# Attention backward of a decode block: dk/dv on the full array, K/V in 8 KB rows, and SP's queue ordered as loads, stores, zeros

## The chip, the core and the metric

The kernel runs on one core of a Trainium2 chip. The metric is the device time in microseconds. Five engines take part: PE (TensorE), DVE (VectorE), ACT (ScalarE), POOL (GpSimd) and SP (SyncE). Each runs its own instructions in order, and each but PE and DVE also issues transfers here, which 16 DMA engines carry out.

## The reference

The reference is the forward pass and all gradients of one decode step: windowed attention with a cache, in parallel with a GEGLU feed-forward block, both on the layer-normed x. There are 4 rows (B = 4), D = 512, 32 query heads over 8 K/V heads of 128, a cache of 4096 positions of which the last W = 1024 are used, F = 1792. Everything is bf16.

```python
xn = layernorm(x)
q = (xn @ wq) per head;  k, v = cache[:, :, Sk-W:], each shared by 4 heads
p = softmax(q k^T / sqrt(128));  o = p v
out = x + o @ wo + (gelu(xn @ w_gate) * (xn @ w_up)) @ w_down
# and the vjp with grad_out: dx, dk_cache, dv_cache, dwq, dwo, dw_gate, dw_up, dw_down
```

The outputs make the traffic. dk_cache and dv_cache (out_2, out_3) have the full 4096 positions: 3072 of each are zeros, 48 MiB in all, and 1024 are computed, 16 MiB in all. K and V are read over 1024 positions (16 MiB), and the weights and their gradients add the rest. The profile counts 30.93 MB read and 81.01 MB written.

## The kernel before

The kernel works in two parts. First comes the feed-forward block (lines 479 to 628): gate, up and down weights are loaded whole, `hg_ps` and `da_ps` are computed, then a loop of 14 steps (the df loop, L614 to L626) transposes the gate and up weights for dx. Then the attention runs in NT = 4 stages of GP = 2 K/V heads each, with 8 query heads for 4 rows, hence 32 pairs of row and head.

A stage t (the loop of L632) goes so. `pre(t)` transposes wo, computes q and the gradient of o, and writes them into `qm` and `dom`, in which each block has the columns of one row and K/V head and zeros elsewhere. `masks(t)` makes masked copies of the two as rows for the outer products (POOL). `scores(t, 0)` transposes K in blocks of 8 x 128x128, copies each block from PSUM with one DVE operation of 1024 columns, and adds up the scores S on 128 partitions: 4 quarters of the window by 32 pairs. `softmax(t)` follows; then `scores(t, 1)` does the same with V and gives dP. `softmax_d(t)` makes dS. `odq` multiplies P by V and dS by K. `fin(t)` transposes wq and adds to the sums for out and dx.

The outer products are cut into pieces that wait in a list `bg`: a piece is one or two matmuls into one PSUM bank and one evacuation of 512 columns. `tick(n)` takes n pieces off the list, between transposes. `dvdk(t, k)` puts 16 pieces for dv or dk on the list, `dw(t)` 16 for dwo and dwq; the feed-forward block leaves 46. In a piece of dk/dv (L406) the contraction runs over one quarter, 32 of the 128 rows of the array. `evac` shares the evacuations between ACT and DVE by a running sum of costs.

Transfers: SP issues x, dy, the feed-forward weights, wo and wq of stages 0 and 1, K/V of stage 0 and half of stage 1, and then `zeros()`: all 32 transfers of 1.5 MiB of zeros, each held until the second before it has landed. ACT issues the later K/V and wo/wq loads (`load_next`, `load_w`), between its evacuations. POOL issues the stores. K and V lie in the tiles as [128 positions mod 8, row, 8 positions, 128], so a partition takes 2 KB from each of the 4 rows. Only SP's order is written by hand (`manual_schedule`); the order of the other engines is a scheduler's.

PSUM pools are `ps_w` (4 banks, shared by transposes, pieces and sums), `ps_a` (S, dP and od) and `ps_x` (1 bank). The staging tiles of dk/dv are 4, those of the other gradients (`outp`) 3.

Of the kernel before, what the change touches and what calls it, by code (L numbers as in the profile page):

```python
# [9 lines left out]
ACT = mybir.ActivationFunctionType  # L10
# [4 lines left out]
P = 128  # L15
# [3 lines left out]
def kernel(  # L19
# [23 lines left out]

    nc = tc.nc
# [11 lines left out]
    J = W // P  # L56
# [3 lines left out]
    RG = B * HG  # L60
    NQ = P // RG
    WQ = W // NQ
    JQ = J // NQ
    NS = B * GP
    CW = HG * Dh
    assert Sq == 1 and Dh == P and D == 512 and F % P == 0 and RG == 32 and JQ * NQ == J and WQ == JQ * P
# [4 lines left out]
    kvp = ctx.enter_context(tc.tile_pool(name="kvp", bufs=3))  # L71
    wres = ctx.enter_context(tc.tile_pool(name="wres", bufs=2))
    attw = ctx.enter_context(tc.tile_pool(name="attw", bufs=2))
    tsb = ctx.enter_context(tc.tile_pool(name="tsb", bufs=5))
# [4 lines left out]
    ctx.enter_context(tc.manual_schedule(engines={nc.sync.engine}))  # L79
# [14 lines left out]
    def store(eng, out, in_, kind, apart):  # L94

        d = eng.dma_start(out=out, in_=in_)  # L96
        for k in apart:
            tc.declare_no_dep(d.ins, group=k, reason="stores write disjoint parts of the outputs")
        tc.add_to_no_dep_group(kind, d.ins)
        return d  # L100


    RB = P // B
    x_b = const.tile([P, D], BF16, name="x_b")
    dy_b = const.tile([P, D], BF16, name="dy_b")
    for dst, src in ((x_b, A_x), (dy_b, grad_out)):
        nc.sync.dma_start(out=dst[:], in_=bass.AP(tensor=src.tensor, offset=src.offset,
                                                  ap=[[D, B], [0, RB], [1, D]]))

    ident = const.tile([P, P], BF16, name="ident")  # L110
    make_identity(nc, ident[:])
    ident_f = const.tile([P, P], FP32, name="ident_f")
    nc.vector.tensor_copy(out=ident_f[:], in_=ident[:])
    one_f = const.tile([1, 1], FP32, name="one_f")
    nc.vector.memset(one_f[:], 1.0)

    msk_i = const.tile([P, rep], FP32, name="msk_i")
    nc.vector.reduce_sum(out=msk_i[:], in_=ident_f[:].rearrange("p (b r) -> p r b", b=B)[:, 0:rep, :], axis=AX.X)


    rsum = const.tile([P, NQ, RG], FP32, name="rsum")
    nc.gpsimd.memset(rsum[:], 1.0)

    msk_f = const.tile([P, GP, B], FP32, name="msk_f")
    nc.gpsimd.memset(msk_f[:], 1.0)
    for q in range(NQ):
        rs = slice(q * RG, (q + 1) * RG)
        nc.gpsimd.affine_select(out=rsum[rs], in_=rsum[rs], pattern=[[0, NQ], [-1, RG]],
                                compare_op=ALU.is_equal, fill=0.0, base=0, channel_multiplier=1)
        nc.gpsimd.affine_select(out=msk_f[rs], in_=msk_f[rs], pattern=[[-rep, GP], [-HG, B]],  # L130
                                compare_op=ALU.is_ge, fill=0.0, base=0, channel_multiplier=1)
        nc.gpsimd.affine_select(out=msk_f[rs], in_=msk_f[rs], pattern=[[rep, GP], [HG, B]],
                                compare_op=ALU.is_ge, fill=0.0, base=rep - 1, channel_multiplier=-1)
    msk = const.tile([P, GP, B], BF16, name="msk")
    nc.vector.tensor_copy(out=msk[:], in_=msk_f[:])

    ZW = K0 // P * Dh
    ztile = const.tile([P, ZW], BF16, name="ztile")
    nc.vector.memset(ztile[:], 0.0)

    qm_all, dom_all = [], []
    for i in range(2):
        for lst, nm in ((qm_all, "qm"), (dom_all, "dom")):
            t_ = const.tile([P, NS, RG + rep], BF16, name=f"{nm}{i}")
            nc.gpsimd.memset(t_[:], 0.0)
            lst.append(t_)


    acc = const.tile([P, 2, ND, B], FP32, name="acc")
    nc.vector.memset(acc[:], 0.0)  # L150

# [3 lines left out]
    def acc_sum(o, terms):  # L155

        ps = ps_w.tile([P, ND, B], FP32, name="acc_ps", tag="w")
        for c in range(ND):
            for k, (lf, rhs) in enumerate(terms):
                nc.tensor.matmul(ps[:, c, :], lhsT=lf(c), rhs=rhs, start=(k == 0), stop=(k == len(terms) - 1))  # L160
        acc_add(o, ps[:])


    od_ps = ps_a.tile([P, 2, GP, Dh], FP32, name="od_ps")
    nc.vector.memset(od_ps[:], 0.0)


    stats = const.tile([P, nc.vector.BN_STATS_DIM], FP32, name="stats")
    nc.vector.bn_stats(out=stats[:], in_=x_b[:])
    mv = const.tile([P, nc.vector.BN_AGGR_DIM], FP32, name="mv")  # L170
    nc.vector.bn_aggr(out=mv[:], in_=stats[:])
    eps_t = const.tile([P, 1], FP32, name="eps_t")
    nc.vector.memset(eps_t[:], eps)
    rstd = const.tile([P, 1], FP32, name="rstd")
    nc.scalar.activation(out=rstd[:], in_=mv[:, 1:2], func=ACT.Sqrt, bias=eps_t[:], scale=1.0)
    nc.vector.reciprocal(out=rstd[:], in_=rstd[:])
    xn_f = const.tile([P, D], FP32, name="xn_f")
    nc.vector.tensor_scalar(out=xn_f[:], in0=x_b[:], scalar1=mv[:, 0:1], scalar2=rstd[:, 0:1],
                            op0=ALU.subtract, op1=ALU.mult)
    xn_b = const.tile([P, D], BF16, name="xn_b")  # L180
    nc.vector.tensor_copy(out=xn_b[:], in_=xn_f[:])

    xnT = const.tile([P, ND, B], BF16, name="xnT")
    dyT = const.tile([P, ND, B], BF16, name="dyT")
    for src, dstT in ((dy_b, dyT), (xn_b, xnT)):
        tps = ps_x.tile([P, ND, P], BF16, name="tps", tag="x")
        for c in range(ND):
            nc.tensor.transpose(tps[:, c, :], src[:, c * P:(c + 1) * P], ident[:])
        nc.vector.tensor_copy(out=dstT[:], in_=tps[:].rearrange("p c (b r) -> p c b r", b=B)[:, :, :, 0])


    xnm = const.tile([P, rep, D], BF16, name="xnm")
    dym = const.tile([P, rep, D], BF16, name="dym")
    for src, dst in ((dy_b, dym), (xn_b, xnm)):
        for i in range(rep):
            nc.vector.tensor_scalar(out=dst[:, i, :], in0=src[:], scalar1=msk_i[:, i:i + 1], scalar2=None,
                                    op0=ALU.mult)


    wo_v = A_wo.rearrange("(t h p) n -> t p h n", p=P, h=HG)  # L200
    wq_v = A_wq.rearrange("(c p) (t j) -> t p c j", p=P, j=CW)
    wo_t, wq_t, k_t, v_t = {}, {}, {}, {}

    def load_w(t, eng):
        wo_t[t] = wres.tile([P, HG, D], BF16, name="wo_sb", tag="wo")
        eng.dma_start(out=wo_t[t][:], in_=wo_v[t])
        wq_t[t] = wres.tile([P, ND, CW], BF16, name="wq_sb", tag="wq")
        eng.dma_start(out=wq_t[t][:], in_=wq_v[t])  # L208

    def load_kv(t, k, g, eng):  # L210
        d_, src, nm = ((k_t, A_k_cache, "kb"), (v_t, A_v_cache, "vb"))[k]
        tl = kvp.tile([P, B, J, Dh], BF16, name=nm, tag=nm)
        eng.dma_start(out=tl[:].rearrange("p b j d -> p b (j d)"),  # L213
                      in_=src[:, t * GP + g, K0:Sk, :].rearrange("b (m j) d -> m b (j d)", j=J))
        d_[(t, g)] = tl

    def load_next(t, k):

        if t + 1 < NT:
            load_kv(t + 1, k, 1, nc.scalar)  # L220
        if t + 2 < NT:
            load_kv(t + 2, k, 0, nc.scalar)


    ZG = 2
    zlist = [(og, b, g) for b in range(B) for g in range(0, G, ZG) for og in (out_2, out_3)]

    def zeros():

        zsrc = bass.AP(tensor=ztile.tensor, offset=ztile.offset, ap=[list(ztile[:].ap[0]), [0, ZG], [1, ZW]])  # L230
        done = []
        for og, b, g in zlist:
            z = store(nc.sync, og[b, g:g + ZG, 0:K0, :].rearrange("g (m j) d -> m g (j d)", m=P), zsrc, "zeros",
                      ["rest"])
            if len(done) >= 2:
                tc.add_manual_dep(z.ins, done[-2].ins.name,
                                  mybir.DependencyInfo(mybir.DependencyClass.Sync, mybir.DependencyReason.DATA))
            done.append(z)
# [7 lines left out]


    st = {}

    def pre(t):  # L250

        wo_sb, wq_sb = wo_t[t], wq_t[t]
        dq_ps = ps_x.tile([P, 2, HG, B], FP32, name="doq_ps", tag="x")
        for h2 in range(HG // 2):
            wT_ps = ps_w.tile([P, 2, ND, P], BF16, name="woT_ps", tag="w")
            for i in range(2):
                for c in range(ND):
                    nc.tensor.transpose(wT_ps[:, i, c, :], wo_sb[:, 2 * h2 + i, c * P:(c + 1) * P], ident[:])  # L258
            woT = tsb.tile([P, 2, ND, P], BF16, name="woT", tag="wT")
            evac(woT[:], wT_ps[:], 1024, half=True)  # L260
            for i in range(2):
                for c in range(ND):
                    nc.tensor.matmul(dq_ps[:, 0, 2 * h2 + i, :], lhsT=woT[:, i, c, :], rhs=dyT[:, c, :],
                                     start=(c == 0), stop=(c == ND - 1))
            tick(2)
        for h in range(HG):
# [445 lines left out]
```

## Time and profile before

| what | value |
|---|---|
| median of 3 runs | 316.91 us (312.36 to 318.90) |
| span of the profiled execution | 311.7 us |
| PE, DVE, ACT, POOL busy | 224.1, 146.3, 113.4, 51.3 us |
| mean clock granted to TensorE | 0.738 of full speed |
| moved by DMA | 112.38 MB, mean 361 GB/s over the span |
| q1 (SP), q10 (ACT), q0 (POOL) | 66.59, 14.69, 30.67 MB |

The profiled execution has no time of its own beside its span; what lies around it is seen from the fastest run, 0.7 us above the span, and the slowest, 7.2 us above it. An engine's busy share is an average over stages with different limits. What ends last is read from the slices of the span, from stretches with their DMA rate and clock, and from the chain of waits. A clock of 0.50 means that matmuls in that stretch took about twice as long.

### The profile page before, as it was taken

Reading aid. Unit: us, or ns where it says so; the run is one execution under the profiler, and the core shown is the slowest. Engines: PE = TensorE matmul, PEld = TensorE weight load, DVE = VectorE, ACT = ScalarE, POOL = GpSimd, SP = SyncE. Lnnn points to the kernel's source line nnn. Section 1 sums busy time; section 2 is a strip of 40 time slices with the busy share of each in tenths; the row PEclk is TensorE's granted clock in tenths of the full one; section 3 lists DMA queues with packets and bytes.
Section 4 is the critical chain, followed back from the end, with each engine's and each line's share of the span. In section 5 each row is a group of like instructions: output and inputs, shape, how many; then the busy total and the mean of one; then the engine's idle time right before and its main releaser. Section 6 shows DMA issues by size and latency. Waiting matters only on the chain.

```text
span 311.7 us, 6831 instructions
## 1 busy us (share of the span) xinstructions
PE 224.1 (72%) x2950; PEld 144.7 (46%) x2956; DVE 146.3 (47%) x304; ACT 113.4 (36%) x217; POOL 51.3 (16%) x76
## 2 busy tenths in 40 slices
PE   1269986936988379779648069969789755979861
PEld 0259874615555244465425044455556333756231
DVE  5246663523743234537414025546545424564766
ACT  3010645613613045346022044435244414533650
POOL 6000121610100005201000004201000501110140
PEclk9998998875975555779955555679955559895585
DMA  5999999999999999999999999998999999431494
GB/s 167 397 351 385 374 402 416 416 422 424 419 295 392 418 374 418 421 420 419 375 418 414 357 418 416 421 420 346 394 410 405 418 422 418 159 145 62 181 335 160
DMA packets 34405, 112.38 MB, mean 361 GB/s; under 512 B 1664, under 2 KB 7816, under 8 KB 34376
## 3 DMA queue, kind: packets, MB, share of 16 engines
q1 hardware_dynamic: 18136, 66.59, 53.6%
q0 software_dynamic: 7808, 30.67, 24.8%
q10 hardware_dynamic: 8432, 14.69, 13.6%
q8 instruction: 23, 0.38, 0.5%
q14 instruction: 6, 0.05, 0.0%
HBM read 30.93 MB, written 81.01 MB: 359 GB/s over the span
## 4 chain that ended last, share of the span: by engine, by line
PE 39%; DMA 30%; ACTq 9%; DVE 8%; issue 6%; ACT 4%; POOL 1%; SPq 1%; DVEq 0%; POOLq 0%
PE T_ps L306 11%; DMA kb<-in_A_k_cache_dram 10%; PE kv_ps L406 7%; ACTq L208 6%; DMA wd_sb<-in_B_w_down_dram 6%; DMA out_dram<-osb_o 5%; DMA vb<-in_A_v_cache_dram 5%; PE S_ps L311 4%; ACTq L213 3%; DMA out_dram<-osb_d 3%; DMA out_dram<-osb_g 2%; PE dwo_ps L426 2%; PE wgT_ps L619 2%; PE wdT_ps L546 2%; PE wqT_ps L471 2%
## 5 line engine op out<-in xcount | busy, mean ns | idle before, releaser
L92 DVE COPY T_sb<-T_ps 128x1024 bf16<-128x1024 bf16 x64 | 44.2, 691 | 41.5 <-PE T_ps L306 40.9
L91 ACT CAST stg_dk<-kv_ps 128x512 bf16<-128x512 f32 x46 | 25.0, 590 | 47.0 <-issue 26.9
L91 ACT CAST stg_dv<-kv_ps 128x512 bf16<-128x512 f32 x52 | 28.2, 590 | 31.9 <-PE kv_ps L406 22.7
L306 PE MATMUL T_ps<-ident,kb 128*128 128x128 bf16 x256 | 32.9, 280 | 6.1 <-DMA kb<-in_A_k_cache_dram 5.0
L406 PE MATMUL kv_ps<-qmr,dS_b 32*128 32x512 bf16 x64 | 23.1, 598 | 16.9 <-ACT stg_dk L91 16.4
L306 PEld LDWEIGHTS <-kb 128*128 128x128 bf16 x256 | 23.0, 125 | 22.2 <-issue 13.3
L306 PE MATMUL T_ps<-ident,vb 128*128 128x128 bf16 x256 | 26.6, 242 | 0.2
L406 PE MATMUL kv_ps<-domr,P_b 32*128 32x512 bf16 x64 | 18.6, 476 | 5.9 <-DVE wqT L92 3.0
L306 PEld LDWEIGHTS <-vb 128*128 128x128 bf16 x256 | 19.0, 109 | 8.0 <-issue 4.8
L91 ACT CAST osb_g<-dwg_ps 128x384 bf16<-128x384 f32 (+1 forms) x30 | 14.4, 534 | 17.2 <-DMA out_dram<-osb_g 5.9
L92 DVE COPY woT<-woT_ps 128x1024 bf16<-128x1024 bf16 x16 | 11.1, 691 | 20.2 <-PE woT_ps L258 20.2
L92 DVE CAST stg_dk<-kv_ps 128x512 bf16<-128x512 f32 x18 | 12.1, 686 | 16.8 <-PE kv_ps L406 16.6
L258 PEld LDWEIGHTS <-wo_sb 128*128 128x128 bf16 x128 | 11.4, 127 | 17.5 <-issue 17.2
L91 ACT CAST osb_o<-dwo_ps 128x512 bf16<-128x512 f32 x23 | 12.8, 587 | 17.1 <-PE dwo_ps L426 15.3
L91 ACT CAST osb_q<-dwq_ps 128x512 bf16<-128x512 f32 x25 | 13.6, 589 | 13.8 <-PE dwq_ps L441 9.2
L92 DVE COPY wqT<-wqT_ps 128x1024 bf16<-128x1024 bf16 x16 | 11.1, 691 | 15.7 <-PE wqT_ps L471 15.7
L96 POOL DMA_DIRECT2D out_dram<-stg_dv x8 | 6.0, 754 | 72.9 <-ACT stg_dv L91 41.8
L258 PE MATMUL woT_ps<-ident,wo_sb 128*128 128x128 bf16 x128 | 15.5, 285 | 1.3 <-DVE stg_dk L92 0.8
L471 PEld LDWEIGHTS <-wq_sb 128*128 128x128 bf16 x128 | 11.1, 129 | 10.5 <-issue 10.5
L471 PE MATMUL wqT_ps<-ident,wq_sb 128*128 128x128 bf16 x128 | 14.8, 287 | 0.8 <-DVE stg_dv L92 0.8
L96 POOL DMA_DIRECT2D out_dram<-stg_dk x8 | 6.1, 767 | 54.6 <-ACT stg_dk L91 42.5
L91 ACT CAST osb_d<-dwd_ps 128x512 bf16<-128x512 f32 x14 | 8.1, 586 | 14.3 <-PE dwd_ps L580 13.4
(182 smaller groups left out, 349.3 us busy)
## 6 DMA issues: line engine op xcount, KB each, us to landing
out_dram<-ztile SPq DMA_DIRECT2D x32, 1536.0 KB, 11.2
out_dram<-stg_dv POOLq DMA_DIRECT2D x8, 1024.0 KB, 11.5
out_dram<-stg_dk POOLq DMA_DIRECT2D x8, 1024.0 KB, 12.4
vb<-in_A_v_cache_dram ACTq DMA_DIRECT2D x5, 1024.0 KB, 15.8
kb<-in_A_k_cache_dram ACTq DMA_DIRECT2D x5, 1024.0 KB, 26.0
out_dram<-osb_o POOLq DMA_DIRECT2D x8, 512.0 KB, 10.4
out_dram<-osb_q POOLq DMA_DIRECT2D x8, 512.0 KB, 4.7
out_dram<-osb_g POOLq DMA_DIRECT2D x8, 448.0 KB, 7.4
```

Source lines behind the costliest of these rows:

```text
L91: return nc.scalar.copy(out=out, in_=in_)
L92: return nc.vector.tensor_copy(out=out, in_=in_)
L96: d = eng.dma_start(out=out, in_=in_)
L208: eng.dma_start(out=wq_t[t][:], in_=wq_v[t])
L213: eng.dma_start(out=tl[:].rearrange("p b j d -> p b (j d)"), in_=src[:, t * GP + g, K0:Sk, :].rearrange("b (m j) d -> m b (j d)", j=J))
L258: nc.tensor.transpose(wT_ps[:, i, c, :], wo_sb[:, 2 * h2 + i, c * P:(c + 1) * P], ident[:])
L306: nc.tensor.transpose(T_ps[:, j, :], blks[(t, g)][:, b, j, :], ident[:])
L311: nc.tensor.matmul(ps[q * RG:(q + 1) * RG, :], lhsT=lf[:, s * RG:(s + 1) * RG], rhs=T_sb[:, q * WQ:(q + 1) * WQ], start=(g == 0 and b == 0 ...
L406: nc.tensor.matmul(mps[:].rearrange("p b d -> p (b d)"), lhsT=src[rs, jj * P:(jj + 1) * P], rhs=mr[rs, g].rearrange("p b d -> p (b d)"), s ...
L426: nc.tensor.matmul(mps[:], lhsT=o_r[:, g, :], rhs=dym[:, i, :], start=True, stop=True)
L471: nc.tensor.transpose(wT_ps[:, i, c, :], wq_sb[:, c, h * Dh:(h + 1) * Dh], ident[:])
L546: nc.tensor.transpose(wT_ps[:, i, c, :], wd_sb[:, 2 * f2 + i, c * P:(c + 1) * P], ident[:])
```

## The change

All engines now run in program order (`manual_schedule` for the five of them). The parts:

1. K and V are laid out as [32 position groups x 4 rows, 32 positions, 128], so a partition takes 8 KB of one row. A score step takes 8 of the 32 positions of one head (`kv_steps`), and the scores of the 4 rows are separate column groups, with T_sb read at a step of 4 elements. S has partitions (row, head, quarter).
2. `spread` writes P and dS as [128, 256 x 4], times a mask that leaves only the partition's own row. It takes the place of P_b and dS_b, and also scales by the softmax sum. With it a dk/dv piece contracts over all 128 partitions at once. P and dS then need 8 transposes each instead of 2, and `odq` has 16 columns of weights per matmul on two column groups, not 4 columns on four.
3. `softmax` and `softmax_d` are cut into links of a list `chain`. `link()` runs one of them after half of a score step or of a `pre` step. `pre(t+1)` moves into stage t, between the two `odq`.
4. SP issues all K/V loads (`load_kv(t + 2, ...)` after the `odq` that frees the tiles), all dk/dv stores, and the zeros: two at the start of the attention, one behind each dk/dv store, four after the last stage's `dw`, the rest after all pieces. Each zero takes 12 KB rows from `ztile`, which is twice as wide, and none waits for another zero by hand. POOL issues wo/wq, w_down and the other stores. ACT issues only the last two small stores.
5. K/V of stage 1 and the second wo/wq set go into the memory of the feed-forward weights once these are read (`kv_b`, `w_b`). Staging tiles of dk/dv are 3.
6. Feed-forward: x and dy are loaded as 4 rows and spread by a matmul (`spread_rows`); the transposes of step n+1 stand ahead of the matmuls of step n; the df loop takes two pieces per step instead of one; weights w_gate, w_up and wq are read with 4 neighbouring rows per partition.

In the new order on SP, two zeros follow the first K/V loads, then come K/V of stage 1, then per stage V(t+2), (dv, zero) x 2, K(t+2), (dk, zero) x 2. Four zeros stand between the last dv store and the last dk stores, beside the ones behind each store, and ten at the end. At most eight of SP's transfers are in flight: each reuses the semaphore of the eighth before it.

The core of the diff:

```diff
-    ctx.enter_context(tc.manual_schedule(engines={nc.sync.engine}))
+    ctx.enter_context(tc.manual_schedule(engines={e.engine for e in (nc.sync, nc.tensor, nc.vector, nc.scalar,
+                                                                     nc.gpsimd)}))
...
-    def zeros():
...
-            if len(done) >= 2:
-                tc.add_manual_dep(z.ins, done[-2].ins.name,
-                                  mybir.DependencyInfo(mybir.DependencyClass.Sync, mybir.DependencyReason.DATA))
...
+    def zero(n=1):
+        for _ in range(min(n, len(zlist))):
+            og, b, g = zlist.popleft()
+            store(nc.sync, og[b, g:g + ZR, 0:K0, :].rearrange("g (m j) d -> m g (j d)", m=P // ZR), ztile[:], "zeros")
...
+    def load_kv(t, k):
...
+        for g in range(GP):
+            tl = kv_pool[t % 2].tile([P, JB, Dh], BF16, name=nm, tag=nm)
+            nc.sync.dma_start(out=tl[:].rearrange("p j d -> p (j d)"),
+                              in_=src[:, t * GP + g, K0:Sk, :].rearrange("b (m j) d -> m b (j d)", j=JB))
...
+    def kv_steps(t, k, links):
...
+        def mm(g, q, T_sb):
+            c0 = SL - 1 - (g * NQ + q)
+            for b in range(B):
+                nc.tensor.matmul(ps[b * RB:(b + 1) * RB, :], lhsT=zt[:, b * GP + g, c0:c0 + RB],
+                                 rhs=T_sb[:].rearrange("p (x b) -> p b x", b=B)[:, b, :], start=(g == 0 and q == 0),
+                                 stop=(g == GP - 1 and q == NQ - 1), tile_position=(0, b * RB))
...
+                evac(T_sb[:], T_ps[:].rearrange("p j x -> p (j x)"), 1024, half=True)
+                tick(1)
+                link(links)
+                if last:
+                    mm(*last)
+                last = (g, q, T_sb)
+                tick(1)
+                link(links)
...
+    def spread(src, rr, nm):
+        out = attw.tile([P, WQ, B], BF16, name=nm, tag=nm)
+        nc.vector.scalar_tensor_tensor(out=out[:], in0=src[:].unsqueeze(2).broadcast_to([P, WQ, B]),
+                                       scalar=rr[:, 0:1], in1=mskb[:].unsqueeze(1).broadcast_to([P, WQ, B]),
+                                       op0=ALU.mult, op1=ALU.mult)
...
-                nc.tensor.matmul(mps[:].rearrange("p b d -> p (b d)"), lhsT=src[rs, jj * P:(jj + 1) * P],
-                                 rhs=mr[rs, g].rearrange("p b d -> p (b d)"), start=True, stop=True,
-                                 tile_position=(q * RG, 0))
+            nc.tensor.matmul(mps[:].rearrange("p q d -> p (q d)"), lhsT=src[:, j * P:(j + 1) * P],
+                             rhs=mr[:, g].rearrange("p q d -> p (q d)"), start=True, stop=True)
...
+                store(nc.sync, og[:, t * GP + g, K0:Sk, :].rearrange("b (m j) d -> m b (j d)", j=JB),
+                      stg[:].rearrange("p j d -> p (j d)"), "rest")
+                zero()
...
+        zero(2)
+        load_w(1)
+        for k in range(2):
+            load_kv(1, k)
+        pre(0)
         for t in range(NT):
-            pre(t)
-            masks(t)
-            scores(t, 0)
+            kv_steps(t, 0, 0)
             softmax(t)
-            dvdk(t, 0)
-            scores(t, 1)
+            kv_steps(t, 1, 1)
+            link(len(chain))
             softmax_d(t)
-            dvdk(t, 1)
+            link()
             odq(t, 0)
-            load_next(t, 1)
+            load_kv(t + 2, 1)
+            if t + 1 < NT:
+                pre(t + 1)
+            link(len(chain))
+            odT(t, 0)
             odq(t, 1)
-            load_next(t, 0)
+            load_kv(t + 2, 0)
+            tick(2)
+            odT(t, 1)
             fin(t)
             if t + 2 < NT:
-                load_w(t + 2, nc.scalar)
+                load_w(t + 2)
             dw(t)
+        zero(4)
         tick(len(bg))
+        zero(len(zlist))
```

## The prediction

> **What bounds the kernel now.** I read the slices of the span first, then the table of stretches, then the chain. In the slices, the DMA share is full until slice 34 of 40 and falls away only then; the row of PEclk alternates between full and half speed.
>
> ```profile
> PE   1269986936988379779648069969789755979861
> ...
> PEclk9998998875975555779955555679955559895585
> DMA  5999999999999999999999999998999999431494
> GB/s 167 397 351 385 374 402 416 416 422 424 419 295 392 418 374 418 421 420 419 375 418 414 357 418 416 421 420 346 394 410 405 418 422 418 159 145 62 181 335 160
> ```
>
> So there are two regimes: to 265 us the 16 DMA engines are the bound (104.3 of the 112.4 MB, mean 394 GB/s), and in the last 46.7 us compute is, with DMA at 173 GB/s. The table of stretches shows both, and what the clock does (columns: busy us of each engine, clock, DMA share, GB/s):
>
> ```profile
> 44.30:88.00 43.70, 30.73 (x398) 19.96 (x399) 20.48 (x43) 18.86 (x40) 9.56 (x12) 0.84 1.02 407
> 152.00:195.00 43.00, 26.43 (x279) 15.22 (x279) 12.95 (x24) 10.61 (x21) 5.24 (x4) 0.54 1.03 407
> 265.00:311.70 46.70, 34.24 (x409) 20.01 (x407) 28.21 (x53) 20.67 (x38) 7.62 (x10) 0.72 0.47 173
> ```
>
> The full queues stall compute early on. The chain in order of time has DMA and ACT's own queue on it wherever K, V or a weight is fetched: ACT issues those loads, and its casts wait behind them.
>
> ```profile
> 86.75 14.70 DMA vb<-in_A_v_cache_dram
> 101.48 8.80 ACTq L208
> ...
> 152.75 8.86 ACTq L213
> ...
> 170.52 10.91 ACTq L208
> ...
> 222.29 30.32 DMA kb<-in_A_k_cache_dram
> ```
>
> The zeros fill the queues to 256.5 us; when they end, stage 3 of the attention still has to be computed. Whoever reorders the zeros trades an early stall against a late drain. Last, the rate of pure drain and a dense stretch at half clock:
>
> ```profile
> 104.00:108.00 4.00, 1.01 (x8) 0.84 (x8) 1.06 (x2) 0.00 (x0) 0.00 (x0) 0.50 1.02 418
> 116.00:120.00 4.00, 4.00 (x31) 2.04 (x30) 1.76 (x4) 2.15 (x4) 2.71 (x2) 0.50 1.03 418
> 140.00:144.00 4.00, 3.85 (x44) 2.17 (x42) 3.12 (x6) 2.25 (x5) 1.24 (x2) 1.00 1.02 425
> ```
>
> **What the skill says.** (1) "TensorE: Matmul & The Clock Gate", Part 1: an idle window drops the array to half clock, a busy one restores it. Here idle does drop it, but busy alone doesn't restore it: at 116 to 120 us PE has no idle time and stays at 0.50, while its dk matmuls use 32 of 128 rows; it recovers about 4 us after the first 128x512 dwo matmuls. (2) "DMA: Bandwidth & Descriptors", Where 436 GB/s comes from: ceiling 435 GB/s. The trace tops out at 428, and at 424 in a slice. (3) Same page, Issuing engines are not separate DMA queues: moving a DMA to another issuer gains no bandwidth, only sequencer time. The trace agrees: 391 to 411 GB/s whichever queue issues. (4) "SBUF — State Buffer", Door 1: within a 16-byte line, strided bf16 reads are free. The score matmuls now read T_sb at a step of 8 bytes; no run shows this yet.
>
> **The change part by part.**
>
> *DMA bytes and rate.* The bytes stay at about 112.1 MB (x and dy are read once, 0.25 MB less). Rows grow from 2 to 8 KB (K, V) and from 6 to 12 KB (zeros). Zeros-heavy slices already run at 416 to 424; I use 424, bounds 418 and 435. Costed at no gain on the critical path except in the drain below. The DMA floor is 112.1/0.424 = 264 us plus start and end.
>
> *FFN.* The first matmuls on wd start at 20.9 us before; the same bytes come first on SP and POOL side by side, so I keep 20.9. Seven iterations of one 0.69 us copy (0.72 apart) instead of the round trip: to 26.8. Then two row_ps evacuations (2 x 0.69) and 13 small operations at 0.21 stand on DVE before the df loop, where before most were done beside da: to 31 (was 29.2). The df loop runs two pieces per step instead of one. At full clock the trace has 8 transposes 0.44 apart, a 512-column matmul 0.22, eight df matmuls 0.21: 1.09 on PE, but two ACT casts of 0.586 make 1.2. 14 x 1.2 + 0.5 + 2 us of waits for an osb buffer: 50.5 (was 44.3). pre(0) with its 10 pieces: 4 x 1.35 + 1.2 + 2.4 = 9: 59.5.
>
> *SP's program order.* After K/V(0) and two zeros SP stands at K(1), which waits for the FFN weights' last reader. Behind it stand K, V(1) and then V(2), which waits for PE anyway at about 80 us; stage 1 needs K(1) at about 98, so this wait is covered by 40 us. If the cover went, 4.2 MB = 10 us would show. What is lost is DMA time: zeros no longer fill 40 to 80 us.
>
> *ACT freed.* All K/V loads go to SP and wo/wq to POOL, where dk/dv's 16 issues of 0.76 us leave. On POOL load_w(t+2) waits for fin(t)'s last read of the weights; behind it stand stage t's dwo/dwq stores, which come later in PE's order too, so nobody waits longer. On SP the loads of V and K(t+2) wait for odq's last read, and dk/dv stores and zeros stand behind them; those stores are evacuated later than that in program order. The 8.8 + 8.9 + 10.9 us of ACT's queue and the 14.7 and 30.3 us DMA waits on the chain go. Next late is PE itself.
>
> *A stage at full clock.* Score step: 0.44 transposes + 2 x 0.22 full-array dk/dv pieces + 0.22 scores = 1.1 on PE; evacuations are 0.73 + 0.3 (DVE) and 0.85 (ACT), 4 PSUM buffers; before runs 1.24 at its best. I take 1.25, bounds 1.1 and 1.45. Sixteen steps 20, plus linked softmax: spread is one DVE operation of 1024 elements. Nearest row: SCALAR_TENSOR_TENSOR, 512 in 748 ns and 256 in 484, so 1.28 us; bounds 0.7 (packed) and 1.4. With 8 transposes and a 0.69 copy it leaves 2.5 us on PE's path, where the unlinked softmax left 4.4 (130.5 to 134.9). odq: 64 matmuls on two column groups instead of four, 1.9 each (was 1.05; bounds 1.1 and 3.5). pre(t+1) with dS spread inside 8.2, odT and two pieces 1.1, fin 0.83 + 4 x 1.2 + 1.3 = 6.9. osb waits 1.5 (before: 4.5 in three). Sum 22 (16 steps less the empty ones, with softmax) + 3.8 + 8.2 + 1.1 + 6.9 + 1.5 = 43.5. Stage 0 has few pieces to run: 38.5.
> 59.5 + 38.5 + 2 x 43.5 = 185.
>
> *Last stage.* To the last dv store: 22 + 1.5 + 1.9, the softmax gradient now uncovered 3.6, odq and the rest 3.0, fin until piece 16 5.5: 37.5, so 222.5. Clock: I allow one half-speed stretch of about 2.6 us in each stage, 1.3 us each, 5 in all: 227.5.
>
> *Drain.* zero(n) hangs on the dk/dv stores: 2 early, 12 in stages 0 to 2 and 1 with stage 3's first dv store, so behind the last dv store SP still issues 17 of 32 zeros (26.7 MB), two dk (2.1), with four dwo/dwq (2.1) beside and itself 1.05: 32.0 MB / 0.424 = 75.5 us, plus 2 to land: 305. All remaining compute (31 pieces, the output rows) lies under it.
>
> 305 is against a span of 311.7. The timed runs lie 0.7 to 7.2 us above that span, the median 5.2: 310 against 316.9, 2.2% less. The runs can tell about 2% from no change.
>
> **The rivals.** *A, the chain above*: 310; its own range 302 to 319 (step 1.15 to 1.35).
>
> *B, DMA floor*: steps at 1.1, spread packed, no cold clock. Then stages are 40 us, shorter than their 18.9 MB (44.5 us), the queues never run dry after 80 us, and the end is 264 + 3 (start) + about 20 idle (40 to 80 us) + 2 = 290 span, 295. For it: the warm spacings of 0.44, 0.22; against: DVE has 33 of 40 us to do in order.
>
> *C, the clock stays low, slower*: place: score steps, pre and fin of every stage. A cold step costs 0.9 + 0.86 + 0.33 = 2.1 against 1.25, a cold fin step 1.8 against 1.2. With half of the score steps and pre and fin cold a stage is 11 us longer; half of that is my price: 5.5 x 3.9 stages = 21, less the 5 allowed: 326. It decides above +13 us, 3.3 us per stage on top of the 1.3 allowed; at 0.5 us lost per cold microsecond that is 9.2 of 43.5 us cold, a mean clock below about 0.89 between 60 and 225 us. For it: 0.54 in the stretches of before; against: full-array pieces in every step now, as in the df loop, whose steps stayed at 0.87 us from 34 to 44 us.
>
> *D, no change as such*: K/V or stores late in SP's one queue, every DMA waiting for the eighth before it. A stage's bursts of 12 MB in 19 us stand 10 us in the queue; three stg buffers cover about 18. Price 4 us per stage: 323 or a little over.
>
> **How the numbers follow.** A 0.50 (0.27 faster by over 2%, that is under 310.6; 0.23 within), B 0.15 (faster), C 0.30 (0.02 within), D 0.05 (0.01 within). Faster 0.42, same 0.26, slower 0.32. The range runs from B's 293 to 333, C with two thirds of the stage cold.
>
> **What would show it.** Right: zeros and stores alone in the last 70 us at 418 to 430 GB/s with PE idle; a dip of DMA between 40 and 80 us; no load on ACT's queue; the last stg_dv store at 220 to 235; clock 0.9 between; df loop ending at 50. Wrong: the last stg_dv store after 240 (C, or DVE), DMA full to the end from 80 us (B), PE waiting for K or V (D), a score step over 1.45, or a drain under 410 GB/s.

## The result, and the profile after

The changed kernel takes 355.37 us (median of 4 runs, 352.51 to 357.33), against 317.08 us for the kernel before in the same runs. The ratio is 1.136, with a 95% interval of 1.123 to 1.148: it is slower by 12 to 15%. Each ratio here compares only the executions in the faster of the two states that runs of one kernel can fall into, so it can differ by some tenths of a per cent from the quotient of the medians beside it. The profiled execution took 357.33 us with a span of 355.6 us. The prediction was 310.0 with a range of 293 to 333.

The slices of the span of the changed kernel, to be set beside those of the kernel before (PE's busy tenths, its clock, the DMA share, GB/s):

```profile
PE   0326978538799990698993499995969802000000
PEclk9999696956999997579998569999599975555555
DMA  7999575993019999928999945998106999999997
GB/s 253 398 394 409 233 243 202 348 400 121 20 35 341 417 409 418 423 93 270 423 415 423 422 178 230 379 421 335 61 0 252 422 393 402 411 433 422 422 427 315
```

Two things are as predicted. In the attention PE is at full clock where it is dense, but for the slices just behind a hole (9, 16 to 17, 23, 28), and from slice 32 on (counted from 0) it is all but idle while DMA drains. But DMA falls away five times and not once (slices 4 to 6, 9 to 11, 17, 23 to 24, and 28 to 29), and PE has holes in slices 8, 15, 21 to 22 and 27. A hole of PE comes ahead of one of DMA: what isn't computed isn't stored. The chain that ended last names what stands in the holes. These are its pieces on stores of `osb` tiles (the staging tiles of the pool `outp`; the last letter tells the gradient, d for dwd, g for dwg and dwu, o for dwo, q for dwq), in order of time (start, length, what it waited for); the last one lies under the drain:

```profile
47.89 7.39 DMA out_dram<-osb_d
63.80 16.91 DMA out_dram<-osb_g
127.58 16.24 DMA out_dram<-osb_o
183.82 15.61 DMA out_dram<-osb_o
237.68 9.31 DMA out_dram<-osb_o
282.62 11.54 DMA out_dram<-osb_o
```

Such a piece runs from the issue of a store to its landing, so the engine's own wait is shorter. The table of waits has the wait, and it belongs to ACT, which is about to write into the tile that the store still reads (total us, times, longest; DVE, which takes some of the evacuations, has two such waits of 21.0 us in all on `osb_o`):

```profile
ACT osb_q L97 <- DMA out_dram<-osb_o: 35.9, 4, 10.9
ACT osb_g L97 <- DMA out_dram<-osb_g: 13.4, 2, 9.1
```

ACT runs in program order, so all its other evacuations stand behind that one, the PSUM banks stay full, and PE stops: two of its longest waits, 9.9 and 10.6 us, are on ACT's and DVE's `osb_q` evacuations. POOL's timeline shows the rhythm in the stage that starts near 120 us (start, length, instruction, and in brackets POOL's idle time before it):

```profile
127.58 0.76 POOL L103 DMA_DIRECT2D out_dram<-osb_o  x1 [7.21 <-ACT osb_o L97]
130.20 0.76 POOL L103 DMA_DIRECT2D out_dram<-osb_o  x1 [1.86 <-ACT osb_o L97]
133.40 0.71 POOL L103 DMA_DIRECT2D out_dram<-osb_q  x1 [2.44 <-DVE m L377]
147.47 0.72 POOL L103 DMA_DIRECT2D out_dram<-osb_q  x1 [13.36 <-ACT osb_q L97]
```

A tile is filled and stored every 2.6 to 3.2 us. The pool has three, so the fourth tile of a stage is wanted 5.8 us after the first store was issued, and that store takes 16.24 us to land. The fourth store comes 14.1 us after the third; where nothing waits (below, with five tiles) this gap is 2.57 us. The stop is 11.5 us. In the kernel before, the second and third stores of that stage were issued 8.5 us apart (131.35 and 139.81 us), so that the fourth tile was wanted 11.8 us after the first store, which landed in 10.4 us at the median.

The median landing of those stores is in the list of transfers (size, us from issue to landing), beside that of the zeros:

```profile
out_dram<-ztile SPq DMA_DIRECT2D x32, 1536.0 KB, 19.6
out_dram<-osb_o POOLq DMA_DIRECT2D x8, 512.0 KB, 15.9
out_dram<-osb_q POOLq DMA_DIRECT2D x8, 512.0 KB, 10.0
```

The last dv store is issued at 274.15 us instead of the 227.5 of the prediction, and the drain starts there (from the stretches: length, then busy us of PE, its weight loads, DVE, ACT and POOL, clock, DMA share, GB/s):

```profile
274.70:355.60 80.90, 10.69 (x53) 4.49 (x49) 14.03 (x25) 9.30 (x17) 2.93 (x4) 0.58 0.98 405
300.00:350.00 50.00, 0.00 (x0) 0.00 (x0) 1.73 (x3) 0.00 (x0) 0.00 (x0) 0.50 1.01 423
```

So of the 50.6 us by which the span is longer than predicted (355.6 against 305), 46.7 lie ahead of the last dv store and 3.9 in the drain.

### The profile page after: what moved, and what is told of

Its sections match the earlier page's. It is cut to its first block, busy times and chain, and to the rows that moved or that the text cites. A ratio compares the mean times of both kernels' runs of the same rounds, so it can differ in the third digit from the quotient of the medians.

```text
span 355.6 us, 6848 instructions
## 1 busy us (share of the span) xinstructions
PE 211.7 (60%) x2960; PEld 145.4 (41%) x2970; DVE 159.0 (45%) x311; ACT 117.4 (33%) x219; POOL 46.7 (13%) x62
## 2 busy tenths in 40 slices
DMA packets 15662, 112.13 MB, mean 315 GB/s; under 512 B 1664, under 2 KB 1680, under 8 KB 7184
## 4 chain that ended last, share of the span: by engine, by line
PE 39%; DMA 28%; DVE 10%; issue 4%; ACT 3%; POOL 0%; ACTq 0%; DVEq 0%; POOLq 0%
DMA out_dram<-osb_o 15%; DMA wd_sb<-in_B_w_down_dram 7%; PE kv_ps L471 7%; PE T_ps L273 6%; DMA out_dram<-osb_g 5%; PE od_ps L444 4%; PE S_ps L339 4%; PE acc_ps L250 2%; PE wqT_ps L273 2%; DMA out_dram<-osb_d 2%; PE wgT_ps L273 2%; PE pT_ps L273 2%; PE woT_ps L273 2%; DVE dS_s L361 1%; DVE P_s L361 1%
## 5 line engine op out<-in xcount | busy, mean ns | idle before, releaser
L97 ACT CAST stg_dk<-kv_ps 128x512 bf16<-128x512 f32 x47 | 25.4, 590 | 11.9 <-PE kv_ps L471 10.6
L504 PE MATMUL dwq_ps<-od_r,xnm 128*128 128x256 bf16 x64 | 12.5, 298 | 24.4 <-ACT osb_q L97 13.6
L471 PE MATMUL kv_ps<-domr,P_s 128*128 128x512 bf16 x60 | 23.9, 414 | 0.0
L98 DVE CAST osb_q<-dwq_ps 128x512 bf16<-128x512 f32 x9 | 6.1, 691 | 35.9 <-DMA out_dram<-osb_o 21.0
L273 PE MATMUL T_ps<-ident,kb 128*128 128x128 bf16 x256 | 21.8, 234 | 0.2 <-issue 0.2
L97 ACT CAST osb_g<-dwg_ps 128x512 bf16<-128x512 f32 (+1 forms) x26 | 13.2, 535 | 23.8 <-DMA out_dram<-osb_g 13.4
L471 PE MATMUL kv_ps<-qmr,dS_s 128*128 128x512 bf16 x63 | 19.6, 379 | 0.5 <-ACT stg_dk L97 0.2
L323 POOL TENSOR_TENSOR domr<-r,msk 128x1024 bf16<-128x1024 bf16 x4 | 7.6, 1890 | 65.6 <-DVE r L320 65.6
L98 DVE COPY wgT<-wgT_ps 128x1024 bf16<-128x1024 bf16 x14 | 9.6, 689 | 8.2 <-PE wgT_ps L273 8.2
L339 PE MATMUL S_ps<-T_sb,qm 128*32 128x256 bf16 x128 | 12.7, 387 | 0.6 <-DVE T_sb L98 0.5
L339 PE MATMUL S_ps<-T_sb,dom 128*32 128x256 bf16 x128 | 12.8, 390 | 0.0
## 6 DMA issues: line engine op xcount, KB each, us to landing
wq_sb<-in_A_wq_dram POOLq DMA_DIRECT2D x4, 1024.0 KB, 19.3
out_dram<-osb_o POOLq DMA_DIRECT2D x8, 512.0 KB, 15.9
```

Of the source, the lines that this page charges most:

```text
L97: return nc.scalar.copy(out=out, in_=in_)
L98: return nc.vector.tensor_copy(out=out, in_=in_)
L273: nc.tensor.transpose(ps[:, i, :], a, ident[:])
L323: nc.gpsimd.tensor_tensor(out=mr[:].rearrange("p g q d -> p (g q) d"), in0=r4[:, k, :].unsqueeze(1).broadcast_to([P, SL, Dh]), in1=msk[:]. ...
L339: nc.tensor.matmul(ps[b * RB:(b + 1) * RB, :], lhsT=zt[:, b * GP + g, c0:c0 + RB], rhs=T_sb[:].rearrange("p (x b) -> p b x", b=B)[:, b, :] ...
L471: nc.tensor.matmul(mps[:].rearrange("p q d -> p (q d)"), lhsT=src[:, j * P:(j + 1) * P], rhs=mr[:, g].rearrange("p q d -> p (q d)"), start ...
```

## The experiments

All are edits of the changed kernel but one. The theories are named by letters, of which only C means what it meant in the prediction: Q (the stores stand behind weight loads in POOL's queue), S (the engines give SP's long rows the larger share), B (three tiles are too few), C (PE's clock). R and D are told where they come up.

### The weights of stages 1 to 3 on SP's queue

```diff
-        nc.gpsimd.dma_start(out=wo_t[t][:], in_=wo_v[t])
+        eng.dma_start(out=wo_t[t][:], in_=wo_v[t])        # wq the same; POOL for stage 0, SP for the others
...
         zero(2)
-        load_w(1)
         for k in range(2):
             load_kv(1, k)
+        load_w(1, nc.sync)
...
-                load_w(t + 2)
+                load_w(t + 2, nc.sync)
```

> The changed kernel with one edit: the loads of wo and wq for stages 1 to 3 are issued by SP (behind K and V of the same stage) and not by POOL; the stores of the weight gradients stay alone on POOL's queue. In the changed kernel PE stops for 7.4, 16.9, 16.2, 15.6 and 9.3 us on the landing of osb stores. Theory Q (the stores stand behind 2 MB of weight loads in POOL's queue, which explains why the three long stalls follow a weight load and the two short ones don't): the three long stalls fall to under 9 us each, last stg_dv store some 22 us earlier (about 252), time about 333. Theory S (SP's queue with its 8 and 12 KB rows takes most of the DMA engines' time whenever it is backlogged, whatever else stands in POOL's queue): the stalls stay within 4 us, since the same bytes are only moved to the queue that wins; time 350 to 358. Theory C (PE's clock, not the stores): no change, 355.

Measured: 336.63 us, ratio to the kernel before 1.074 (1.070 to 1.078), 19 us less than the changed kernel. Its chain:

```profile
48.17 7.43 DMA out_dram<-osb_d
59.93 8.80 DMA out_dram<-osb_g
117.32 11.59 DMA out_dram<-osb_o
168.92 10.25 DMA out_dram<-osb_o
217.16 9.32 DMA out_dram<-osb_o
```

The three pieces that followed a weight load fell by 8.1, 4.7 and 5.4 us, the other two stayed. Q has the right sign and nearly the size; two of the pieces stay above its 9 us. C, which expected no change, is out as the cause.

### Zeros in rows of 6 KB

```diff
-    ZW = K0 * Dh * ZR // P
+    ZW = K0 * Dh * ZR // P // 2
+    zsrc = bass.AP(tensor=ztile.tensor, offset=ztile.offset, ap=[list(ztile[:].ap[0]), [0, 2], [1, ZW]])
...
-            store(..., og[b, g:g + ZR, 0:K0, :].rearrange("g (m j) d -> m g (j d)", m=P // ZR), ztile[:], "zeros")
+            store(..., og[b, g:g + ZR, 0:K0, :].rearrange("g (m j) d -> m g (j d)", m=P), zsrc, "zeros")
```

> The changed kernel with one edit: each zero transfer has the same 1.5 MB, place and order, but is made of 6 KB rows (256 of them) as in the kernel before, in place of 128 rows of 12 KB. Theory S (engines take one row in turn from each queue, so the queue with the longer rows gets the larger share): POOL's 4 KB rows get 4 of 10 instead of 4 of 16 beside zeros; landing of osb_o falls from 15.9 to about 11 us, the stalls by a third, time about 335. Theory Q (order inside POOL's queue): landing and time change by less than 1.5%, 350 to 360.

Measured: 350.18 us (ratio 1.118, 1.112 to 1.125), 5 us less. The interval touches that of the changed kernel (1.123 to 1.148), so the time alone is weak evidence; the trace is better. The landing of osb_o fell from 15.9 to 12.4 us and the pieces of 16.24 and 15.61 us to 12.93 and 12.30; those in the feed-forward part, where few zeros flow, stayed at 7.21 and 16.62. S is at work, but at a quarter of the price I gave it (5 us of 20). K, V and dk/dv kept their 8 KB rows; whether that is why was not tried.

### No zeros

```diff
-        for _ in range(min(n, len(zlist))):
+        for _ in range(0):
```

> The changed kernel without any of the 32 zero transfers (left out: the zero rows of dk and dv ahead of the window, 50.3 of 112.1 MB); all else in place. What ends last is then the compute: 302 us in the changed kernel, of which 11.5 us is the last stall on an osb store. Theory S: without zeros POOL's stores land in under 8 us, all stalls together fall from 77 to under 20 us, end about 240 to 250. Theory Q: the stalls behind weight loads stay above 8 us each, end 265 to 280. Theory C (compute itself slower than I worked out): over 285.

This kernel leaves out the zero rows of dk and dv. Measured: 276.13 us (ratio 0.874, 0.866 to 0.882), inside Q's range. The median landing of osb_o fell to 6.3 us, as S had it, but without any zeros the chain still has a piece of 16.56 us on osb_g and two of 10.16 and 9.43 us on osb_o, all three behind a weight load. So the zeros account for about 6 of the 16 us in a stage. With 62 of 112 MB to move the changed kernel was still at 276 us.

### The stores on ACT's own queue

```diff
-                store(nc.gpsimd, out_5[r0:r0 + rep * Dh, :]...
+                store(nc.scalar, out_5[r0:r0 + rep * Dh, :]...     # and the stores of out_4, out_6, out_7, out_8
```

> The changed kernel with one edit: the 28 stores of dwd, dwg, dwu, dwo and dwq are issued by ACT on its own queue, which carries nothing else, in place of POOL's. It costs ACT 28 issues and waits for DVE's last copy. Theory Q: the stores no longer stand behind weights; long stalls fall below 9 us, time 328 to 338. Theory S: landing stays at 12 us or more, time 345 to 358. A theory that POOL's queue as such is slow [...]: landing as short as in the kernel before (under 8 us) in all five stalls, time under 320.

Measured: 354.18 us (ratio 1.130, 1.126 to 1.134), no gain. The pieces on osb_o are 17.83, 16.82 and 9.96 us though nothing else is in the queue. Q alone doesn't explain this, and there is no sign that POOL's queue as such is slow. The packets of each queue in four microseconds do (queue, packets, MB, share of the engines' time), first at 123 to 127 us of the changed kernel, then at 127 to 131 us of this one (q1 is SP's queue, q0 POOL's, q10 ACT's):

```profile
q1 hardware_dynamic: 110, 1.18, 70.2%
q0 software_dynamic: 115, 0.47, 29.2%
```

```profile
q1 hardware_dynamic: 137, 1.00, 60.1%
q0 software_dynamic: 127, 0.48, 29.8%
q10 hardware_dynamic: 135, 0.14, 10.1%
```

The numbers of packets are nearly equal, the bytes are not. That is what comes out if every queue with work gets one packet in turn. SP's packets have 8 or 12 KB, POOL's 4 KB, and the same stores cut for ACT's queue have 1 KB. ACT's queue therefore moved 0.14 MB in 4 us, 35 GB/s, where POOL's had 118. The Trainium skill states the rule in "DMA: Bandwidth & Descriptors", Queues, rings and completion order: each engine takes turns between the queues that have work, a packet at a time. The counts agree with it, if what the profile counts as a packet is what the page means by one. With zeros in 6 KB rows the same four microseconds of the second experiment gave

```profile
q1 hardware_dynamic: 171, 1.01, 61.7%
q0 software_dynamic: 168, 0.63, 39.1%
```

so POOL's queue had 158 GB/s instead of 118. Q and S are thus two factors of one number: a store lands after the bytes ahead of it in its own queue, divided by that queue's share. As a test of size: 2.1 MB of weights and 0.5 MB of the store at 118 GB/s are 22 us. POOL's queue moved its first bytes at 121 us, which gives 143; the store landed at 143.8.

### Four tiles in place of three

```diff
-    outp = ctx.enter_context(tc.tile_pool(name="outp", bufs=3))
+    outp = ctx.enter_context(tc.tile_pool(name="outp", bufs=4))
```

> The changed kernel with one edit: the pool of osb tiles has 4 buffers in place of 3. A stage of the attention fills 4 osb tiles (two osb_o, two osb_q) and the next stage's first one comes over 40 us later, so with 4 no stage reuses a tile of its own. Theory B (three buffers and a late landing are the whole of the loss; the landing may stay as late as it is): the stalls of 16.2, 15.6, 9.3 and 11.5 us in the attention vanish, those of 7.4 and 16.9 in the FFN's stores shrink by the 2 to 5 us that one more tile gives; last stg_dv store near 230 instead of 274, time 305 to 315. Theory R (the stall is where a full DMA queue shows first; without it the next buffer, stg, T_sb or K/V, waits as long): osb stalls vanish from the chain, but stg or K/V stand in their place, time above 335. Theory C (PE's clock): 350 or more.

Measured: 320.97 us (ratio 1.023, 1.016 to 1.029), 34 us less. ACT's four waits on osb_o are gone from the table, the last dv store is issued at 238.31 us, and landing is on the whole not shorter (osb_o 13.5 us against 15.9, osb_q 18.5 against 10.0). What is left on osb stores is in the feed-forward part, as before:

```profile
47.42 7.55 DMA out_dram<-osb_d
60.13 17.16 DMA out_dram<-osb_g
```

I had said 305 to 315: the attention's part is right, but I gave the feed-forward stalls 2 to 5 us of relief and they had none. R (the next buffer waits as long) appears only in small: the chain now runs through two stg_dv stores (16.04 and 13.60 us from issue to landing), but ACT waits 3.5 us in all for a stg tile (a staging tile of dk or dv) and DVE 2.1. The drain is as long as before, 81 us from the last dv store to the end of the span.

### Zeros moved ahead, three tiles

```diff
-        zero(2)
+        zero(8)
         load_w(1)
         for k in range(2):
             load_kv(1, k)
+        zero(8)
```

> The changed kernel with 3 osb buffers, and zeros moved in SP's order alone: 8 instead of 2 ahead of K(1), and 8 behind V(1), where SP stands from 62 to 104 us and the DMA engines fall to 35 GB/s; so 14 of the 16 or 17 that drain at the end go early. Theory B with the share by row length: the drain of 81 us after the last dv store falls by about 14 x 3.7 = 52 us to 30, but the early zeros take three quarters of the engines from POOL's stores and weights: the stalls of the FFN's stores (7.4 and 16.9) grow by 5 to 15 us together; time 315 to 330. Theory D (the drain alone is the loss, stalls don't grow): 303. If the compute chain is the limit at the end whatever the zeros do: 302 us of chain less the last stall, 300 to 310.

Measured: 323.66 us (ratio 1.030, 1.023 to 1.038), inside the 315 to 330. The drain shrank to 30 us, as expected, so D (the drain alone is the loss) is out: the stalls in the feed-forward part grew, and by more than the 5 to 15 us that I had expected. In place of 7.39 and 16.91 us the chain has there

```profile
45.90 12.66 DMA out_dram<-osb_d
62.47 10.89 DMA out_dram<-osb_g
75.75 23.32 DMA out_dram<-osb_g
```

The last dv store moved from 274.15 to 293.78 us: 20 us of the gain of 52 us in the drain went back into waits for tiles.

### Four tiles and weights on SP; five tiles and 6 KB zeros

These combine edits already shown; the second has `bufs=5`, for which the narrower zero tile makes room.

> The changed kernel with 4 osb buffers and the weights of stages 1 to 3 on SP's queue (both edits that were named before). Theory B: with the attention's stalls gone only the FFN's stores wait, and there the weights' removal takes the long one from 16.9 to 8.8 or less, as with 3 buffers: 6 to 8 us under the kernel with 4 buffers alone, about 300. If 4 buffers cover the FFN's stores too, or if SP's order delays a weight that PE waits for, the two are equal within 1%.

Measured: 319.09 us (ratio 1.016, 1.009 to 1.022), 2 us less than with four tiles alone, where I had expected 6 to 8. The piece on osb_g fell to 8.83 us, but pre waits for wo and wq behind SP's other transfers, about 2 us a time.

> The changed kernel with 5 osb buffers and zeros in 6 KB rows (the shorter zero tile makes the room); weights stay on POOL's queue. Theory B: in the FFN two more tiles give 4 to 8 us of cover against stalls of 7.2 and 16.6: 5 to 9 us under the kernel with 4 buffers, less what the 6 KB rows give or take (the zeros' rate in the drain was 411 to 416 against 422 to 427 GB/s, 1.5 us over 27 MB): about 300.

Measured: 312.43 us (20 runs, ratio 0.996, 0.992 to 0.999). That is 8.5 us under the kernel with four tiles, as expected (5 to 9); the absolute figure of about 300 carried on the miss made there. No osb store is left on the chain. The last dv store comes 48.5 us earlier than in the changed kernel:

```profile
225.66 0.55 SPq L103 DMA_DIRECT2D out_dram<-stg_dv  x1
```

17 zeros still stand behind that store, 83 us to the end of the span.

### Five tiles and early zeros, and the kernel before with four tiles

The first has `zero(6)` in both places; the second the weights on SP too; the third is the kernel before with `bufs=4` for `outp`.

> The changed kernel with 5 osb buffers, zeros in 6 KB rows, and 6 zeros in place of 2 ahead of K(1) and 6 behind V(1). With 5 buffers and the old places of the zeros compute ended at 242 us and DMA ran alone to 308.8. Theory B with share by row length: early zeros take 6 of 10 parts from POOL's queue between 40 and 85 us, which has 5.5 MB of stores and 2 MB of weights to bring through: 5 buffers don't cover that wholly, FFN stalls of 5 to 15 us come back, the chain ends at 250 to 257, the drain has 10 zeros fewer (15.7 MB, 37 us), end at 280 to 290, set by the 112.1 MB at 415 GB/s (270) plus 5 to 6 us of start and some 10 of gaps. Theory D (drain alone decides, stalls don't return): 275. If the early zeros cost the chain all that they save in the drain, as half of it with 3 buffers: 300 or more.

Measured: 296.30 us, against 314.70 for the kernel before on that chip; there is no interval, for the runs of the kernel before spread there from 305.21 to 317.87. I had expected 280 to 290. A piece on an osb store is back on the chain (11.42 us, in the feed-forward part), as expected, but the larger wait is new: six zeros hold SP's queue ahead of the first dv stores, and DVE stops for a stg tile.

```profile
DVE stg_dk L98 <- DMA out_dram<-stg_dv: 22.7, 1, 22.7
```

> As the one before, and the weights of stages 1 to 3 on SP's queue behind K and V, so that POOL's queue carries stores alone. Theory B: FFN stalls of under 5 us, end 278 to 286, up to 6 us under the one before; against it: with 4 buffers pre waited for wo and wq about 2 us in two stages when they came through SP, so equal within 1% if the FFN's stores are covered anyway.

Measured: 303.53 us, 7 us more than without the weights on SP. I had expected equal or less. ACT's and DVE's wait for stg is 16.9 us, waits of pre for wq and wo are up to 3.7 us, and the DMA rate falls to 331 to 360 GB/s in four slices of the later stages. With the weights on SP's queue the count of packets under 2 KB is 4752 against 1680; that these make the lower rate was not tried by itself.

> The kernel before with 4 osb buffers in place of 3, nothing else. On its own chain, landings of osb stores stand for 8.2, 7.3, 12.0 and 3.7 us. Theory B with zeros as the bound of the kernel before: the stalls shrink by some 15 us, but DMA was full to 265 us all the same (zeros paced on SP fill every gap), so only what stood in the dense last stretch comes back: 2 to 6 us faster, 308 to 313. A theory that the same fault cost both kernels alike: 290 to 300. No effect, since nothing there waited long: 314 within 1%.

Measured: 311.51 us (309.31 to 314.92) against 314.70 (305.21 to 317.87). A gain of more than 2% is not seen; one of 1% can't be told from none. The fault was there in the kernel before but cost it little, and both the slower pace of its tiles and the zeros that fill its gaps may be reasons for that; they weren't parted.

### The zeros where DMA was idle

```diff
-        zero(2)
+        zero(6)
         load_w(1)
         for k in range(2):
             load_kv(1, k)
+        zero(3)
...
             dw(t)
-        zero(4)
+            if t == NT - 2:
+                zero(4)
```

with five tiles and 6 KB zeros.

> The changed kernel with 5 osb buffers, zeros in 6 KB rows, weights on POOL's queue, and the zeros placed by where the DMA engines were idle: 6 ahead of K(1), 3 (not 6) behind V(1), 4 at the start of the last stage, and only what is left at the end. With 6 behind V(1) and none at the last stage's start it took 296.3 us: DVE waited 22.7 us for a stg buffer while six zeros held SP's queue, and the DMA engines stood nearly empty for 14 us before the last dk/dv stores. Theory B: the stg wait falls to under 10 us, the gap of 14 us fills, end 280 to 287, near the floor of 270 us for 112.1 MB at 415 GB/s plus start and landing. If the stalls only move on (stg behind the four late zeros): 290 to 296.

Measured: 285.41 us (284.52 to 286.32), ratio to the kernel before 0.908, interval 0.904 to 0.913, inside the 280 to 287 expected. It is 9% faster than the kernel before and 20% faster than the changed one, with the same arithmetic. Its DMA row has no hole left:

```profile
DMA  6999999999999999999999999999999999999991
GB/s 221 405 390 392 412 422 417 417 395 405 391 423 420 422 407 415 419 421 416 402 332 422 420 411 417 423 418 420 423 407 403 414 414 419 414 405 384 405 396 49
```

The stg wait is down to 7.8 us at its longest. 112.13 MB over 283.7 us is a mean of 395 GB/s.

## Why the prediction was wrong

**The failed step: "osb waits 1.5" for a stage, and "2 us of waits for an osb buffer" in the feed-forward part.** Up to the last dv store they came to 6.5 us in the sum. The experiment with five tiles takes the waits away and brings that store to 225.66 us, so they were worth 48.5. (Of this the 6 KB rows may have a share where no tile is waited for; with 12 KB rows and four tiles it is 35.8 with the feed-forward's waits still in.) I had taken the kernel before's total of 4.5 us in three waits and carried it over. (In its table of waits ACT also has 5.9 and 4.9 us on stores of the feed-forward part, for which I allowed 2.) But a wait for a tile isn't a property of the store: it is the landing time less the time until the tile is wanted again. The change moves both. With two pieces a step of 1.25 us, which the prediction itself uses, four pieces fill a tile in 2.5 us, and the fourth tile is wanted some 5 us after the first store (5.8 measured). The kernel before's landing of 10.4 us alone then gives about 5 us a stage, three times the figure used, and the landing of 16 gives over 10.

**"So nobody waits longer", of the weight loads on POOL's queue.** I looked at the order of instructions and not at the bytes. Two loads of 1 MB ahead of the stores in one queue cost 19 us (the first experiment).

**Rows of 8 and 12 KB "costed at no gain on the critical path".** I asked what longer rows do to the total rate and not to the other queue. Packets taken in turn mean that the queue with longer rows gets more: 5 us from the zeros' rows alone. What the 8 KB rows of K, V, dk and dv cost was not tried by itself. That an issuer is no queue of its own, which the prediction cites from the skill, holds for the sum of the bandwidth and says nothing of its division. The same division would account for the late wd at the start, before any store, though no run tried it: from 5 to 25 us POOL's queue, which now carries wd, had 558 packets with 2.22 MB and SP's 599 with 5.64 MB, and wd landed 23.4 us after its issue, against 17.6 behind the gate and up weights on SP's queue in the kernel before. "I keep 20.9" looked at the bytes that come first and not at that.

**The other terms of the attention's chain stand.** The kernel with five tiles shows them with no wait on an osb store. Stage 0 is 39.5 us from its first transposes of K to the next stage's (predicted 38.5), stages 1 and 2 are 43.2 and 42.8 (43.5 each), and the last one is 36.4 to its last dv store (37.5). A piece of its chain shows the score step; transposes start 1.31 us apart (predicted 1.25), and one `odq` follows:

```profile
122.12 0.45 PE T_ps L274 x8
...
123.43 0.45 PE T_ps L274 x8
...
124.74 0.45 PE T_ps L274 x8
...
126.38 1.78 PE od_ps L445 x64
```

`odq` takes 1.78 (1.9), and `spread` 1.30 in the changed kernel (1.28).

**The strided reads of T_sb are not free.** The prediction put the four score matmuls of a step at 0.22 us, and its fourth point from the skill calls such reads free. At full clock four such matmuls (each on 32 columns of the array, over 256 columns of T_sb) take 0.23 us from their start to the start of the next matmul in the kernel before, which reads T_sb in one run, and 0.33 in the changed one, which reads it at a step of 8 bytes:

```profile
142.15 0.29 PE L311 MATMUL S_ps<-T_sb,dom 128*32 128x256 bf16 x4
142.38 0.39 PE L406 MATMUL kv_ps<-domr,P_b 32*128 32x512 bf16 x1
```

```profile
232.75 0.40 PE L339 MATMUL S_ps<-T_sb,qm 128*32 128x256 bf16 x4
233.08 0.39 PE L471 MATMUL kv_ps<-qmr,dS_s 128*128 128x512 bf16 x1
```

At half clock both take 0.34 us. So the measurement decides against the page, though no run changed the step of the reads alone. By an estimate from these figures it is 0.1 us in each of the 64 score steps, some 6 us of PE's time, and half of the way from the 1.1 us at which the prediction priced PE's part of a step to the 1.31 that PE takes.

**The feed-forward part, and luck.** It came out late: wd arrives at 25.0 us and not at 20.9, and the first transposes of the df loop start at 39.2 and not at 31. The loop itself then takes 18.7 us against 19.3, so it ends at 57.9 and not at 50.5. Two errors cancel this: pre(0) takes 6 us and not 9, and the 5 us allowed for a cold clock aren't needed. Sum: 225.7 against 227.5, and the 227.5 has 6.5 us of waits for osb tiles in it, which this kernel doesn't have. That the sum comes so near is partly luck.

**The drain.** 17 zeros behind the last dv store, PE idle under them: right. 81.5 us to the end of the span against 77.5: the mean was 405 GB/s, with 423 in its middle, and the last slice, at 315, wasn't in my rate. So the sign "a drain under 410 GB/s" came true as well.

**From span to time.** I allowed 5 us around the span. The profiled executions here are 1.7 us over theirs.

**The rivals and the signs.** C, my main case for slower, fell: with five tiles PE's clock is at 0.9 or 1.0 from the first stage to the drain but for one slice of 0.7, and in the changed kernel it falls only with a stall. With full-array pieces it stayed up; whether they or the steadier stream of matmuls keep it was not parted. D of the prediction placed the lateness on SP's queue; in the changed kernel that did PE no harm, and it was POOL's queue, fed by the same 16 engines, that was late. SP's queue came into play only with the osb waits gone and the zeros moved (22.7 us on a stg tile). The sign "last dv store after 240" came true, but I had put it down beforehand to the clock or to DVE. The list of signs had no line for a wait on a store.

## What to carry to other kernels

For every pool of staging tiles (the tiles that wait for their store), compare two times whenever an edit touches either: how soon the tile is wanted again, and how long its store takes to land. When engines run in program order, a single late tile stops all of them; one more tile of 4 KB per partition was worth 34 us here. A store lands after the bytes ahead of it in its own queue, at a rate set by the size of its packets against those of the other busy queues, so keep bulk loads and long zero rows out of the way of stores that compute waits for, and put fill traffic where the DMA row of the profile shows holes.

## What the runs showed of the hardware

Queues with work had nearly equal numbers of packets served, whatever the packets' size: 137, 127 and 135 in four microseconds for three queues whose packets had 7.3, 3.8 and 1.0 KB in the mean. The same stores to rows of 1 KB in memory went out as 4 KB packets from POOL's queue and as 1 KB packets from ACT's, so moving them to a queue of their own made them land hardly earlier (14.0 against 15.9 us at the median), with stalls as long as before.

A matmul that reads bf16 at a step of 8 bytes took as long at full clock as at half clock: four of 256 columns in 0.33 and 0.34 us, where reading in one run took 0.23 and 0.34.
